# Attention-value product of one core: 128-query chunks as two 64-column halves, value tiles with rows of 72 instead of 66 elements

## The chip, the core and the metric

The kernel runs on one core of one Trainium2 chip. The metric is the device time of one execution in microseconds. Before the change it is 365.22 us, the median of three runs (364.77 to 365.48). The profile that is read below is one execution with a span of 363.3 us.

The names of the engines are those of the profile: PE is TensorE's matmul side and PEld its weight loads, DVE is VectorE, ACT ScalarE, POOL GpSimd, SP the queue from which most transfers are issued.

## What is computed

Attention with pooled queries for 8 batches of 8 heads, 1152 positions, head size 64, and behind it a layer with two input matrices, a maximum and an output matrix. In the reference (cut to what matters; `B, H, S, D = 8, 8, 1152, 64`, 4608 pooled tokens):

```python
q_pool = q.reshape(B, H, S // 2, 2, D).mean(axis=3)
scores = np.matmul(q_pool, k.transpose(0, 1, 3, 2)) / np.sqrt(D)
attn = np.exp(scores - np.max(scores, axis=-1, keepdims=True))
attn = attn / (np.sum(attn, axis=-1, keepdims=True) + 1e-09)
attn_out = np.matmul(attn, v)
x = attn_out.transpose(0, 2, 1, 3).reshape(B * 576, H * D)
out = np.maximum(x @ w1, x @ w2) @ w_out
```

## The kernel before, in words

Heads are taken two at a time, which gives 32 pairs (4 per batch). For a pair the 576 pooled queries and the 1152 keys make 9 key tiles of 128 (`NT`) by 576 queries, for each of two heads. Scores are made transposed, keys on the partitions: line 738 multiplies `kT` by `qpT`, two matmuls side by side, one per head, each on 64 rows of the array, into a score tile `sps`. ACT takes the exponential of a group of 512 columns of both heads (line 745) into `et`, in bf16. No maximum is subtracted; the sum of the exponentials comes from a column of ones that stands behind the 64 value columns in `vE`.

The attention-value product of a pair is what the change touches. It is made by `av_jobs` in units of PE work, for each head (`half`):

- `chunk(half, sb)`, line 649: for 128 queries (`sb` from 0 to 3) nine matmuls, one per key tile, added up in PSUM. The stationary operand is a 128x128 piece of `et`, the moving operand the 65 columns of `vE` (64 values and the ones). The result lies on 128 partitions, queries down, 65 columns wide. There are 8 chunks in a pair, 256 in all, so 2304 matmuls.
- `rest()`, line 661: the last 64 queries of both heads. Here the stationary operand is 128x64, the one head writes PSUM partitions 0 to 63 and the other 64 to 127, so two matmuls lie beside each other in the array as two column tiles of 64. 18 matmuls per pair, 576 in all.
- `norm(half)`: DVE takes the reciprocal of the sums (line 671) and multiplies (lines 675 and 679) into `xnat`.

`vE` is filled by a POOL cast (line 549) from the loaded values; a row of it has 66 elements for one head and key tile, of which 65 are read.

PE's other work in the same stretch of time is the maxout layer, whose weights are turned into a difference `wd` and a product `w21`: line 952 (`xT` by `wd`), line 985 (output product, pairs of matmuls on 64 rows each), and at the end lines 925 and 1018, the same products with all 128 rows. Lines 870, 569, 585, 618, 800 and 841 are small products and transposes; lines 464 and 473 are matmuls on a constant that keep PE busy.

A planner places all of this. Its costs and due times make a first order, but what is emitted comes from strings written out by hand, one letter for each unit, one string for each of PE, DVE, POOL and SP (`pe_order` and the others, from line 1577). Every unit waits for the semaphores of what it reads and of the bank that it writes. The planner's modes name how the array is cut up: `f` for the whole array, `s` for two row halves, `c` for two column halves, `z` for quarters. The mode of `chunk` is `f` and that of `rest` is `c`; the change leaves these words and the strings alone.

Of the kernel before, what the change touches and what calls it, by code (L numbers as in the profile page):

```python
# [8 lines left out]
BF16 = mybir.dt.bfloat16  # L9
P = 128  # L10
# [344 lines left out]
def bass_funnel_attn__then__act_maxout2_kernel(  # L355
# [13 lines left out]
    NT = S // P  # L369
    HP = P // 2  # L370
# [23 lines left out]
    with outer:  # L394
        def sbuf(shape, dt, name):
            return room.enter_context(nc.sbuf_tensor(name, list(shape), dt))
# [12 lines left out]
        qpT = [sbuf([P, SQ], BF16, f"qpT{s}") for s in range(3)]  # L409
        kbf = [sbuf([P, NT, 2, D], BF16, f"kbf{s}") for s in range(2)]  # L410
        kT = [sbuf([P, NT, P], BF16, f"kT{s}") for s in range(3)]
        vE = [sbuf([P, NT, 2, 66], BF16, f"vE{s}") for s in range(3)]
        et = sbuf([P, 4 * PW], BF16, "et")
        et2 = et[:, :].rearrange("p (h c) -> p h c", h=2)
        rcs = sbuf([P, NPAIR, 2 * NCH + 1], FP32, "rcs")
# [18 lines left out]
        fb = [w[:, half, :] for w in wide for half in range(2)]  # L434
# [4 lines left out]
        def rows(half):  # L439
            return slice(half * HP, half * HP + HP)  # L440
# [112 lines left out]
        def unit(r, cost, go, mode="f"):  # L553

            def plan_it(m):
                op("PE", lambda e: go(e, m), r=r, w=[f"f{m}"], cost=cost, mode=mode)
            return r, plan_it, cost, mode

        def dve(fn, r, w, cost):
            op("DVE", fn, r=r, w=w, cost=cost)  # L560
# [73 lines left out]
        def av_jobs(i):  # L634
            b, h0 = i // NHP, 2 * (i % NHP)
            es = i % 2
            vs = i % 3
            xs = b % 2
            need = [f"et{es}.{g - first(i)}" for g in range(first(i), after(i))] + [f"vE{vs}", f"v.{i}"]

            def col(half, t, sb):
                return (half * 2 + es) * PW + flat(i, t, sb * P)

            def chunk(half, sb):

                def go(e, m):
                    for t in range(NT):
                        a = col(half, t, sb)
                        last = e.matmul(  # L649
                            fb[m][:, sb * 66:sb * 66 + 65], et[:, a:a + P],  # L650
                            vE[vs][:, t, half, 0:65], start=(t == 0), stop=(t == NT - 1))
                    return last
                return unit(need, 0.2755, go)

            def rest():

                def go(e, m):
                    for t in range(NT):
                        for half in range(2):
                            a = col(half, t, NCH)  # L660
                            last = e.matmul(  # L661
                                fb[m][rows(half), NCH * 66:NCH * 66 + 65], et[:, a:a + NB],
                                vE[vs][:, t, half, 0:65], start=(t == 0), stop=(t == NT - 1))
                    return last
                return unit(need, 0.308, go, "c")

            def norm(half):
                def evac(m):
                    n = NCH + 1 - half
                    a = fb[m][:, 0:(NCH + 1) * 66].rearrange("p (j c) -> p j c", c=66)  # L670
                    dve(lambda e: e.reciprocal(rcs[:, i, half * (NCH + 1):half * (NCH + 1) + n], a[:, 0:n, 64]),  # L671
                        [f"f{m}"], [f"rc{half}"], 0.19)
                    if half == 0:
                        for k in range(2):
                            dve(lambda e, k=k: e.tensor_tensor(
                                xnat[xs][rows(0), i % NHP, NCH, k * D:k * D + D], a[rows(k), NCH, 0:D],
                                rcs[rows(k), i, NCH:NCH + 1].to_broadcast([HP, D]), ALU.mult),
                                [f"f{m}", "rc0"], [f"xr{xs}.{h0 + k}"], 0.221)
                    dve(lambda e: e.tensor_tensor(
                        xnat[xs][:, i % NHP, 0:NCH, half * D:half * D + D], a[:, 0:NCH, 0:D],  # L680
                        rcs[:, i, half * (NCH + 1):half * (NCH + 1) + NCH].unsqueeze(2).to_broadcast([P, NCH, D]), ALU.mult),
                        [f"f{m}", f"rc{half}"], [f"xn{xs}.{h0 + half}", f"f{m}"], 0.425)
                return evac

            return [Job("a", ([] if half else [rest()]) + [chunk(half, sb) for sb in range(NCH)],
                        norm(half), nb=i) for half in range(2)]

        def first(i):

            return i * PW // W  # L690

        def after(i):
            return -(-(i + 1) * PW // W)
# [4 lines left out]
        def flat(i, t, lo):  # L698

            at = 0  # L700
            for a, z in runs(i):
                if lo < z:
                    return at + t * (z - a) + lo - a
                at += NT * (z - a)
# [959 lines left out]
```

## Time and profile before

| | |
|---|---|
| median of 3 runs | 365.22 us |
| span of the profiled execution | 363.3 us |
| PE busy, matmuls | 354.4 us (98%), 5973 |
| PE weight loads | 222.3 us (61%), 5973 |
| ACT busy | 314.7 us (87%) |
| DVE busy | 242.1 us (67%) |
| POOL busy | 124.4 us (34%) |
| granted TensorE clock | 1.000 |

The median lies 1.9 us over the span, which is what the span does not hold of an execution. Matmuls overlap: a matmul of 65 columns is listed with some 0.19 us although the next starts about 0.03 us after it, so the pace of a row of matmuls is read from first start to last start, and not from the mean of one. A row "start, length, xN" of the timeline covers the N instructions from the first start to the end of the last.

### The profile page before, as it was taken

The numbers are of one execution on the slowest core, as the hardware profiler recorded it, in microseconds if no ns is written. First come the engines' busy times: TensorE is split into PE (matmuls) and PEld (weight loads), VectorE is DVE, ScalarE is ACT, GpSimd is POOL, SyncE is SP. The second block draws the span as 40 slices with busy tenths as digits, with TensorE's granted clock in tenths as the row PEclk, the third lists the DMA queues.
The fourth block names the chain that finished last, engine by engine and source line by source line (L and its number), as shares of the span: only waits on it lengthen the run. The fifth ranks groups of instructions, "written<-read, shape, count | busy, mean of one in ns | idle before, by whom it ended". The sixth has DMA issues, their size and how long they took to land.

```text
span 363.3 us, 13384 instructions
## 1 busy us (share of the span) xinstructions
PE 354.4 (98%) x5973; PEld 222.3 (61%) x5973; DVE 242.1 (67%) x526; ACT 314.7 (87%) x355; POOL 124.4 (34%) x111
## 2 busy tenths in 40 slices
PE   7998999999999999999999999999999999999995
PEld 6675655666564666657575665666666566656842
DVE  2777468877589777948968595676977847715421
ACT  4999999989999999999999999999999989894221
POOL 1246986344045433452251604613424320010000
PEclk9999999999999999999999999999999999999999
DMA  7999999999859998996999999986999570723106
GB/s 261 403 395 396 403 278 325 233 311 308 212 98 265 280 291 248 232 267 152 315 297 210 239 298 299 294 258 161 249 252 241 162 163 12 190 47 68 41 6 174
DMA packets 77790, 84.78 MB, mean 233 GB/s; under 512 B 50080, under 2 KB 50848, under 8 KB 77728
## 3 DMA queue, kind: packets, MB, share of 16 engines
q1 hardware_dynamic: 77168, 83.09, 85.8%
q8 instruction: 48, 0.79, 0.9%
q10 hardware_dynamic: 560, 0.79, 0.7%
q14 instruction: 14, 0.11, 0.1%
HBM read 62.91 MB, written 9.44 MB: 199 GB/s over the span
## 4 chain that ended last, share of the span: by engine, by line
PE 89%; ACT 7%; DMA 1%; issue 0%; SPq 0%; POOL 0%; DVE 0%; DVEq 0%
PE sps L738 20%; PE sps L649 13%; PE sps L985 11%; PE fb L985 10%; PE sps L952 9%; ACT et L745 7%; PE fb L649 7%; PE fb L952 7%; PE sps L1018 3%; PE sps L661 2%; PE fb L870 2%; PE fb L1018 1%; PE sps L925 1%; DMA kraw<-in_k_dram 1%; PE fb L661 1%; PE fb L925 1%
## 5 line engine op out<-in xcount | busy, mean ns | idle before, releaser
L745 ACT ACTIVATE et<-sps 128x1024 bf16<-128x1024 f32 (+1 forms) x336 | 306.7, 1006 | 19.7 <-PE sps L738 17.8
L738 PE MATMUL sps<-qpT,kT 64*128 64x256 bf16 (+7 forms) x1162 | 118.4, 283 | 0.7 <-ACT et L745 0.3
L603 DVE STREAM_TRANSPOSE qpT<-qp 32x288 bf16<-32x288 bf16 x216 | 101.4, 469 | 5.6 <-PE sps L738 1.5
L738 PEld LDWEIGHTS sps<-qpT,kT 64*128 64x128 bf16 x1162 | 47.9, 94 | 48.4 <-ACT et L745 16.3
L543 POOL TENSOR_TENSOR qp<-qraw 128x576 bf16<-128x576 f32 x30 | 42.1, 1405 | 89.6 <-DVE qpT L603 66.0
L549 POOL TENSOR_SCALAR vE<-vraw 128x1152 bf16<-128x1152 f32 x32 | 36.8, 1151 | 65.8 <-DMA vraw<-in_v_dram 63.4
L649 PE MATMUL sps<-vE,et 128*128 128x65 bf16 x1368 | 48.6, 193 | 0.4 <-issue 0.4
L649 PEld LDWEIGHTS sps<-vE,et 128*128 128x128 bf16 x1368 | 43.7, 97 | 6.5 <-issue 5.6
L510 POOL TENSOR_SCALAR kbf<-kraw 128x1152 bf16<-128x1152 f32 x31 | 35.6, 1151 | 33.4 <-DMA kT<-kbf 16.8
L952 PE MATMUL sps<-xT,wd 64*128 64x512 bf16 (+3 forms) x368 | 43.4, 326 | 0.0
L985 PE MATMUL sps<-wo,stage 64*128 64x512 bf16 x256 | 36.8, 376 | 0.0
L952 PE MATMUL fb<-xT,wd 64*128 64x512 bf16 (+3 forms) x272 | 33.5, 333 | 0.1
L649 PE MATMUL fb<-vE,et 128*128 128x65 bf16 x936 | 33.1, 193 | 0.0
L985 PE MATMUL fb<-wo,stage 64*128 64x512 bf16 x224 | 33.0, 376 | 0.0
L649 PEld LDWEIGHTS fb<-vE,et 128*128 128x128 bf16 x936 | 29.8, 97 | 4.8 <-issue 4.1
L961 DVE TENSOR_SCALAR stage<-sps 128x1024 bf16<-128x1024 f32 (+3 forms) x23 | 22.3, 969 | 15.4 <-PE sps L952 15.2
L961 DVE TENSOR_SCALAR stage<-fb 128x1024 bf16<-128x1024 f32 (+3 forms) x17 | 17.0, 999 | 10.7 <-PE fb L952 10.4
L952 PEld LDWEIGHTS sps<-xT,wd 64*128 64x128 bf16 x368 | 15.6, 94 | 13.5 <-PE sps L952 1.4
L671 DVE RECIPROCAL rcs<-sps 128x5 f32<-128x5 f32 (+1 forms) x38 | 7.0, 185 | 20.0 <-PE sps L649 19.5
L985 PE MATMUL sps<-w,xT 64*128 64x512 bf16 x128 | 18.8, 376 | 0.0
L996 DVE COPY stage<-sps 128x1024 f32<-128x1024 f32 x8 | 9.8, 1225 | 12.8 <-PE sps L985 12.7
L985 PEld LDWEIGHTS sps<-wo,stage 64*128 64x128 bf16 x256 | 12.1, 94 | 9.5
(88 smaller groups left out, 292.9 us busy)
## 6 DMA issues: line engine op xcount, KB each, us to landing
vraw<-in_v_dram SPq DMA_DIRECT2D x32, 576.0 KB, 6.6
kraw<-in_k_dram SPq DMA_DIRECT2D x31, 576.0 KB, 6.3
qraw<-in_q_dram SPq DMA_DIRECT2D x31, 576.0 KB, 6.1
out_dram<-stage SPq DMA_DIRECT2D x21, 256.0 KB, 5.8
out_dram<-stage SPq DMA_DIRECT2D x23, 128.0 KB, 3.3
xT<-in_moe_w_dram SPq DMA_DIRECT2D x4, 512.0 KB, 10.3
stage<-in_moe_w_out_dram SPq DMA_DIRECT2D x4, 512.0 KB, 14.0
stage<-in_moe_w_dram SPq DMA_DIRECT2D x4, 512.0 KB, 13.7
```

What stands on the lines that cost most here:

```text
L510: op("POOL", lambda g: g.tensor_scalar(kbf[s][:, :, :, :].rearrange("p t h d -> p h t d"), kraw[r][:, :, :, :], 1.0, 1.0, ALU.mult, ALU.mu ...
L543: op("POOL", lambda g: g.tensor_tensor(qpf[s][:, :, :], qraw[r][:, :, 0, :], qraw[r][:, :, 1, :], ALU.add), r=[f"qraw{r}"], w=[f"qp{s}.0", ...
L549: op("POOL", lambda g: g.tensor_scalar(vE[r][:, :, :, 0:D].rearrange("p t h d -> p h t d"), vraw[r][:, :, :, :], 1.0, 1.0, ALU.mult, ALU.m ...
L603: op("DVE", lambda e: e.transpose(view[dst:dst + 32, :, 32 * pb:32 * pb + 32], qpf[s][src:src + 32, :, 32 * db:32 * db + 32]), r=[f"qp{s}. ...
L649: last = e.matmul(fb[m][:, sb * 66:sb * 66 + 65], et[:, a:a + P], vE[vs][:, t, half, 0:65], start=(t == 0), stop=(t == NT - 1))
L661: last = e.matmul(fb[m][rows(half), NCH * 66:NCH * 66 + 65], et[:, a:a + NB], vE[vs][:, t, half, 0:65], start=(t == 0), stop=(t == NT - 1))
L738: last = e.matmul(sps[r][:, h, col:col + hi - lo], kT[i % 3][rows(h), t, :], qpT[i % 3][rows(h), lo:hi], start=True, stop=True)
L745: op("ACT", lambda e: e.activation(et2[:, :, c:c + z - a], sps[r][:, :, a - g * W:z - g * W], EXP, scale=scale), r=[f"s{r}"], w=keys + ([f ...
L952: last = e.matmul(fb[m + k][:, 0:size], wd[z, ct, (f0 + k) * P:(f0 + k + 1) * P], xT[z, ct, n0:n1], start=(turn == 0 and ct == 0), stop=(t ...
L961: dve(lambda e: e.tensor_scalar_max(gT[:, f0:f0 + 2, g0:g0 + size], wide[m // 2][:, :, 0:size], 0.0), [f"f{m}", f"f{m + 1}"], w + [f"f{m}" ...
L985: last = e.matmul(fb[m + k][:, :], lhs, rhs, start=(turn == 0 and j == 0), stop=(turn == 1 and j == NC_ + NF - 1))
L1018: return e.matmul(fb[m][:, 0:c1 - c0], lhs, rhs[:, c0:c1], start=(j == 0), stop=(j == NC_ + NF - 1))
```

## The change

```diff
-        vE = [sbuf([P, NT, 2, 66], BF16, f"vE{s}") for s in range(3)]
+        vE = [sbuf([P, NT, 2, 72], BF16, f"vE{s}") for s in range(3)]
...
                     for t in range(NT):
                         a = col(half, t, sb)
-                        last = e.matmul(
-                            fb[m][:, sb * 66:sb * 66 + 65], et[:, a:a + P],
-                            vE[vs][:, t, half, 0:65], start=(t == 0), stop=(t == NT - 1))
+                        for k in range(2):
+                            last = e.matmul(
+                                fb[m][rows(k), sb * 66:sb * 66 + 65], et[:, a + k * HP:a + k * HP + HP],
+                                vE[vs][:, t, half, 0:65], start=(t == 0), stop=(t == NT - 1))
                     return last
                 return unit(need, 0.2755, go)
```

`HP` is 64 and `rows(k)` is partitions 64k to 64k + 63. Each matmul of a chunk becomes two: the stationary operand is split into two halves of 64 queries, the moving operand is the same for both, and the halves write the lower and the upper 64 partitions of the same columns. The PSUM layout, and so all that DVE reads, stays as it was. A row of `vE` takes 72 elements; 65 of them are read as before. Every line behind the edit has a number one higher.

On PE, early in the program (a rest unit and five chunks of a pair, then scores, then three chunks), the order before was

```order
L661 MATMUL sps<-vE,et 64x65 x18
L649 MATMUL sps<-vE,et 128x65 x45
L738 MATMUL sps<-qpT,kT 128x64 x2
L738 MATMUL sps<-qpT,kT 128x448 x2
L738 MATMUL sps<-qpT,kT 128x128 x2
L738 MATMUL sps<-qpT,kT 128x384 x2
L649 MATMUL sps<-vE,et 128x65 x27
```

and it is now

```order
L662 MATMUL sps<-vE,et 64x65 x18
L650 MATMUL sps<-vE,et 64x65 x90
L739 MATMUL sps<-qpT,kT 128x64 x2
L739 MATMUL sps<-qpT,kT 128x448 x2
L739 MATMUL sps<-qpT,kT 128x128 x2
L739 MATMUL sps<-qpT,kT 128x384 x2
L650 MATMUL sps<-vE,et 64x65 x54
```

Nothing changes places; twice as many matmuls stand in a chunk's row, and they have the shape of the rest's.

On PE near the end, where single matmuls of line 925 (whole array) stand between chunks of the last pair, the order before was

```order
L661 MATMUL sps<-vE,et 64x65 x18
L925 MATMUL sps<-xT,wd 128x128
L649 MATMUL sps<-vE,et 128x65 x45
L925 MATMUL sps<-xT,wd 128x128
L649 MATMUL sps<-vE,et 128x65 x18
L925 MATMUL fb<-xT,wd 128x128
L649 MATMUL sps<-vE,et 128x65 x9
L1018 MATMUL sps<-w,xT 128x512 x3
```

and it is now

```order
L662 MATMUL sps<-vE,et 64x65 x18
L926 MATMUL sps<-xT,wd 128x128
L650 MATMUL sps<-vE,et 64x65 x90
L926 MATMUL sps<-xT,wd 128x128
L650 MATMUL sps<-vE,et 64x65 x36
L926 MATMUL fb<-xT,wd 128x128
L650 MATMUL sps<-vE,et 64x65 x18
L1019 MATMUL sps<-w,xT 128x512 x3
```

Here too the places are the same, but a chunk now has another shape than the matmul of line 926 beside it. The rows of DVE, ACT, POOL and SP, and what they wait for, are the same in both.

## The prediction, as put on record before the run

> **What bounds the kernel now.** I read the page first: the span, the engines' shares and the chain of work that ended last.
>
> ```profile
> span 363.3 us, 13384 instructions
> PE 354.4 (98%) x5973; PEld 222.3 (61%) x5973; DVE 242.1 (67%) x526; ACT 314.7 (87%) x355; POOL 124.4 (34%) x111
> PE 89%; ACT 7%; DMA 1%; issue 0%; SPq 0%; POOL 0%; DVE 0%; DVEq 0%
> ```
>
> A busy PE proves little, since matmuls overlap, but the chain runs over PE for 89% of the span. Where its other 7% lie, the chain in order of time tells:
>
> ```profile
> 7.68 0.67 PE fb L464 x12
> 8.35 0.34 PE sps L738 x4
> 8.69 0.02 issue
> 8.71 26.76 ACT et L745 x30
> 35.47 0.05 issue
> 35.52 0.39 PE sps L738 x4
> 35.91 0.86 PE fb L870 x8
> ...
> 39.65 0.41 PE sps L661 x18
> 40.05 1.46 PE sps L649 x45
> 41.52 0.54 PE sps L738 x8
> 42.06 0.93 PE sps L649 x27
> ```
>
> From 8.7 to 35.5 us the exponentials set the pace and PE waits for them; from 35.9 us on the chain names ACT no more, so PE's order alone sets the end. The waits of PE's matmuls agree:
>
> ```profile
> PE sps L738 <- ACT et L745: 0.3, 2, 0.2
> ```
>
> So there is no slack behind 35.9 us in which a longer PE stretch could vanish: what a chunk gains or loses there goes to the end one for one. Before it, it costs nothing. How many of the chunk matmuls lie on either side (first row before, second behind; PE time, then PEld):
>
> ```profile
> 0.00:35.90 35.90, 5.57 (x144) 4.77 (x144) 1.00 0.97 363
> 35.90:363.30 327.40, 76.16 (x2160) 68.76 (x2160) 1.00 0.86 219
> ```
>
> 240 of the 256 chunks count. The clock granted to PE is 1.00 in both stretches, and I take it to stay there.
>
> **The change part by part.** Nothing changes its place in any engine's order, and no wait is added; the sum is one of PE's pace.
>
> *Today's pace.* The shortest, middle and longest matmul of both kinds, and stretches of the timeline:
>
> ```profile
> L649 PE MATMUL sps<-vE,et x1368: 190/192/204, 40.0 to 334.4; 128*128 128x65 bf16 x196
> L661 PE MATMUL sps<-vE,et x342: 192/195/218, 39.6 to 332.0; 128*64 128x65 bf16 x171
> ...
> 290.30 2.35 PE L649 MATMUL fb<-vE,et 128*128 128x65 bf16 x72
> ```
>
> 72 matmuls take 2.35 us less the last one's 0.19, over 71 steps: 30.4 ns from start to start. Over all: the order of the program has 70 unbroken rows of chunk matmuls on PE, 7 of them in the first 36 us. The 63 others hold 76.16 us less 63 x 0.192, 64.1 us, in 2160 - 63 = 2097 steps: 30.5 ns a step, start-up of a row included.
>
> *The new pace.* The trace already has the new form: the rest unit of line 661 (18 matmuls in two column tiles of 64, 65 moving columns). One of them, cut off after 47.20 us and whole, and the chunk behind it:
>
> ```profile
> 47.14 0.25 PE L661 MATMUL sps<-vE,et 128*64 128x65 bf16 x4
> ...
> 47.14 0.47 PE L661 MATMUL sps<-vE,et 128*64 128x65 bf16 x18
> 47.54 0.24 PE L649 MATMUL sps<-vE,et 128*128 128x65 bf16 x2
> ...
> 35.90:363.30 327.40, 14.22 (x540) 10.95 (x540) 1.00 0.86 219
> ```
>
> The fourth matmul ends at 47.39 and so began at 47.19: the second pair starts 53 ns after the first, a start-up. The 30 rest units behind 35.9 us (last row) hold 14.22 us, 0.474 each, less 0.195 for the last matmul: 0.279 us from first to last start. Less the start-up of 0.053 and the 0.004 that the two of a pair lie apart, 0.222 us remain for 7 pairs: **31.9 ns a pair**, which now does what one step of 30.5 did. A bound from below is today's 30.5; one from above takes the start-up into the pace, 0.275 / 8 = 34.4. I take 31.9, as this is the same instruction, tile and moving size.
>
> - Steps: 2097 x (31.9 - 30.5) = +2.9 us.
> - Start-up: of the 63 rows 23 stand right behind a rest unit, which already has the new form; 40 start anew, 40 x (53 - 32) ns = +0.8 us.
> - Between rest and chunk the array now keeps its form. Today the last rest matmul of the row above starts at 47.415 (47.14 + 0.47 - 0.195) and the chunk at 47.54, 125 ns; from then on 32 - 4 = 28. 23 x 97 ns = -2.2 us. One chunk row stands ahead of a rest unit, -0.1 us.
> - Six borders between chunks and whole-array matmuls become changes of form. Three are these:
>
> ```profile
> 331.68 0.47 PE L661 MATMUL sps<-vE,et 128*64 128x65 bf16 x18
> 332.08 0.23 PE L925 MATMUL sps<-xT,wd 128*128 128x128 bf16 x1
> 332.15 1.52 PE L649 MATMUL sps<-vE,et 128*128 128x65 bf16 x45
> 333.51 0.22 PE L925 MATMUL sps<-xT,wd 128*128 128x128 bf16 x1
> 333.56 0.71 PE L649 MATMUL sps<-vE,et 128*128 128x65 bf16 x18
> 334.11 0.22 PE L925 MATMUL fb<-xT,wd 128*128 128x128 bf16 x1
> 334.17 0.43 PE L649 MATMUL sps<-vE,et 128*128 128x65 bf16 x9
> 334.44 0.81 PE L1018 MATMUL sps<-w,xT 128*128 128x512 bf16 x3
> ```
>
>   From chunk to line 925 it is 0.03 us today (333.56 + 0.71 - 0.19 to 334.11), from rest to line 925 0.12 (331.96 to 332.08): 6 x 0.1 = +0.6 us.
> - The second matmul of the last pair starts 4 to 5 ns later, 58 times ahead of other work: +0.3 us.
>
> The sum is 2.9 + 0.8 - 2.2 - 0.1 + 0.6 + 0.3 = **+2.3 us**, 363.3 to 365.6 us in the profiled execution; the median stood 1.9 us above that span, so 365.2 + 2.3 = **367.5 us**. With the bounds of the pace, 30.5 and 34.4 ns (start-up then within it), the sum is -0.6 and +6.8: 364.6 to 372.0.
>
> Edits at nothing. The padding: POOL casts into rows of `vE` in as much time as into the dense rows of `kbf`, and had 63.4 us of waiting for the loads of `vE` alone, which a slower cast would use up first.
>
> ```profile
> L549 POOL TENSOR_SCALAR vE<-vraw 128x1152 bf16<-128x1152 f32 x32 | 36.8, 1151 | 65.8 <-DMA vraw<-in_v_dram 63.4 <-PE sps L649 2.4
> L510 POOL TENSOR_SCALAR kbf<-kraw 128x1152 bf16<-128x1152 f32 x31 | 35.6, 1151 | 33.4 <-DMA kT<-kbf 16.8 <-DMA kraw<-in_k_dram 13.5 <-PE sps L738 3.0
> q8 instruction: 48, 0.79, 0.9%
> ```
>
> For PE the row length changes the step between key tiles, 264 to 288 bytes, and no count of elements; nothing in the trace prices it, and I let it lie within the bounds of the pace. The 4608 added PE instructions (half matmuls, half loads) have to be fetched: 48 packets serve today's 11946, so some 18 more, a third of a per cent of the DMA engines' time. DVE reads the same PSUM columns.
>
> The trace bears most on the weight load. A load of 64 columns is listed in line 661 just before each matmul, and pairs follow in 32 ns. [...]
>
> **The rivals.**
>
> *A. PE's sequencer can't feed the stream.* A chunk now needs four instructions in 32 ns, 8 ns each. A rest unit shows that pace, but for 36 instructions only, which may have stood ready. The longest dense stretch is that of the fence with line 925: 93 matmuls, 186 instructions from 331.68 to 334.44 us, 14.8 ns each. If PE is fed no faster than that, a pair takes 59 ns. There are 69 unbroken stretches of attention-value work behind 35.9 us, with 2430 pairs; if the first 9 pairs of each go at 32, the other 1809 lose 27 ns each, +49 us on top of the 2.3: 416 us. Feeding at 11.4 ns, halfway, adds 25: 392 us. From 8 ns on it costs nothing. For it: no long stream of this kind stands in the trace. Against it: the 14.8 is what was asked for there, not a limit that was hit. [...]
>
> *B. Loads bind in long rows.* If the 53 ns of the first two pairs came back whenever loads can't be pulled ahead, each pair would cost 53: 2097 x 21 ns more, +44 + 2.3, 411 us. Against it speak all 30 rest units behind their first pair.
>
> *C. Faster.* The two halves of a pair read the same moving row, where a rest's two read different ones, and rows are now 144 bytes apart. If that lets a pair go at 30.0 ns, the steps give -1.0 and the rest of the sum -0.6: 363.6 us. It decides below 30.8 ns, where the steps' loss equals the saved changes of form. For it: today's single step is 30.5 with the same moving columns. Against it: line 569's transposes are pairs of the same kind on dense rows of 64, and 18 of them also took 0.47 us:
>
> ```profile
> 31.23 0.47 PE L569 MATMUL fb<-ident,qp 64*64 64x64 bf16 x18
> ```
>
> *D. No change,* with a pair at 30.5 to 31.2 ns: 364.6 to 365.9 us.
>
> **How the numbers follow.** Forecast, a pair near 32 ns, 366 to 372 us: 0.62. A 0.16, B 0.04, C 0.10, D 0.08. The predicted time is the forecast's, 367.5 us. A difference of 0.2%, 0.7 us, is about what a measurement can tell from none. Faster 0.10, same 0.08, slower 0.82. The range has to reach into A, whose times spread from 372 to 416: 364.2 to 381 us leaves out some 0.07 below (most of C) and 0.14 above.
>
> **What would show it.** Right: a chunk row of 90 matmuls at 1.44 us from first to last start (45 pairs of 32 ns); rest and chunk 28 ns apart instead of 126; ACT still off the chain behind 36 us. A shows as a row whose first pairs come every 32 ns and whose later ones come further apart, the longer the row the worse; B as 53 ns from the second pair on; C as a pair below 31. The step most likely wrong is that a pace read over 9 pairs holds for 45. The forecast falls altogether if ACT or a transfer comes back onto the chain behind 36 us.

## The result, and the profile after

The changed kernel takes 426.85 us, the median of 6 runs (418.33 to 431.74); the kernel before took 365.35 us (6 runs, 364.58 to 369.25). The ratio is 1.153, with a 95% interval of 1.148 to 1.158: 15% slower, where +2.3 us had been forecast. (The ratio leaves out runs more than 1.5% above the fastest of their kernel, the profiled one among them, and so lies below the ratio of the medians, 1.168.)

The page of the changed kernel: span, engines, PE and its granted clock in 40 slices, the queue that brings instructions, the chain of waits, and the groups of the exponentials and the chunks (busy us, mean ns, then idle time ahead of them and what ended most of it).

```profile
span 426.9 us, 17992 instructions
PE 376.8 (88%) x8277; PEld 235.5 (55%) x8277; DVE 242.7 (57%) x526; ACT 318.3 (75%) x355; POOL 124.5 (29%) x111
PE   8877999599899979989949988979797969999996
PEclk9998999889899999999999999989988988999999
q8 instruction: 66, 1.08, 1.1%
PE 84%; issue 10%; DMA 2%; ACT 1%; SPq 1%; DVE 1%; DVEq 0%
L746 ACT ACTIVATE et<-sps 128x1024 bf16<-128x1024 f32 (+1 forms) x336 | 310.3, 1001 | 79.1 <-PE sps L739 77.3
L650 PE MATMUL sps<-vE,et 128*64 128x65 bf16 x2736 | 53.6, 196 | 14.3 <-issue 14.2
L650 PE MATMUL fb<-vE,et 128*64 128x65 bf16 x1872 | 38.1, 199 | 17.9 <-issue 17.9
```

The span grew by 63.6 us, from 363.3 to 426.9. PE is busy for 88% of it in place of 98%, and "issue", time in which it waited for nothing that the profile shows, rose from 0% to 10% of the chain. The chunk matmuls alone lost 32 us to it (the last two rows). The exponentials, in the page of before, were this group:

```profile
L745 ACT ACTIVATE et<-sps 128x1024 bf16<-128x1024 f32 (+1 forms) x336 | 306.7, 1006 | 19.7 <-PE sps L738 17.8
```

They now wait 77.3 us for scores in place of 17.8: ACT waits for PE more than before, and not PE for ACT.

What such an idle time looks like: the timeline of PE around 220 us.

```profile
217.31 0.61 PE L739 MATMUL sps<-qpT,kT 64*128 64x256 bf16 x8
217.85 1.08 PE L650 MATMUL fb<-vE,et 128*64 128x65 bf16 x56
222.48 1.64 PE L650 MATMUL fb<-vE,et 128*64 128x65 bf16 x52 [3.55 <-issue]
224.05 0.61 PE L739 MATMUL sps<-qpT,kT 64*128 64x384 bf16 x4
```

And four stretches there, with PE, PEld, DVE, ACT and POOL busy, then the granted clock, the DMA share and GB/s:

```profile
215.00:218.70 3.70, 3.34 (x124) 2.47 (x125) 0.60 (x2) 1.98 (x3) 0.00 (x0) 1.00 1.26 238
218.80:222.40 3.60, 0.13 (x10) 0.02 (x2) 0.00 (x0) 0.89 (x1) 0.00 (x0) 0.95 1.23 211
222.50:225.40 2.90, 2.90 (x62) 2.12 (x64) 1.18 (x4) 0.70 (x1) 1.15 (x1) 0.50 0.02 6
225.50:231.50 6.00, 6.00 (x70) 2.88 (x66) 3.67 (x10) 5.71 (x7) 0.00 (x0) 1.00 0.01 3
```

PE stops in the middle of a row of chunk matmuls, which need no new data and no semaphore, and stands still for 3.55 us. Then it goes on at a clock of 0.50: 52 matmuls take 1.64 us, where the 56 ahead took 1.08. The clock's record has 0.50 for 3.41 us, from 222.02 us on, and then 1.00 again. So this stop costs twice, and it falls where the DMA share is 1.23.

**Where the stops lie.** I counted PE's instructions (weight loads, matmuls and the few semaphore instructions) in order of their start. Every stop of 0.5 us or more, from one start to the next, inside a row of attention-value matmuls lies at a number 193 + 256k: 705, 1217, 3009, 3265, 9153, 13249, 14273 and so on, and so do the largest stops in other work (8897, in line 986). Six more of 0.5 us or more stand at other numbers and between other lines, five of them ahead of 43 us. The instruction queue q8 moves one packet for each 256 of them: with borders at these numbers PE's 16634 instructions here make 66 blocks and the 12026 of before make 48, as many as q8 has packets (66 for 1.08 MB, 16.4 KB each, and 48), and the 18 that were added are 4608 / 256. I read the stops so that PE stands at the end of a block of 256 because the next has not come: in the four rows of after below it runs on 1.41 to 1.52 us behind the end of the next packet. The table is from the records of q8 and PE (us; "entered" is the first instruction of a block, "stop" the time from the last start ahead of it):

```
            block   entered   next packet     next block
                              begins  ends    entered   stop
after         961    27.83     31.64  32.68     34.12    3.47
after        3009    77.21     81.06  82.00     83.41    3.64
after        8897   215.36    219.95 220.96    222.48    3.74
after       14017   343.80    347.48 348.67    350.13    4.31
before       1473    43.06     46.40  47.55     49.56    0.58
before       2497    73.04     76.45  77.56     79.13    none
```

In the profile of after 30 blocks come late, with 0.3 us or more at their borders. On the mean of these, 2.72 us pass from a block's entry to the first byte of the next packet, 1.10 us while it arrives, and 1.41 us until PE runs on (1.19 to 1.56 in all 30): 5.23 us, with 3.00 to 7.14 in single blocks. PE used these 30 up in 2.03 to 6.52 us, from first start to last, and then stood for 0.34 to 4.31 us. A block that is all chunks now holds 64 pairs at 32 ns, 2.0 us; of the old form it would have held 128 matmuls at 30.5 ns, 3.9 us, and mixed with scores and maxout the old blocks lasted from 5.6 to some 10 us. The kernel before lived just above the 5.23 us. The one stop of 0.58 us in its profile stands at such a number, but this account does not cover it: its packet had landed 2.01 us before PE ran on, longer than in any of the 30, and the run with the padding alone (below) has no stop there.

The bill of the 63.6 us, in starts over all block borders: 50.5 us at borders now, 2.5 before, **48.0**. The clock is 0.50 for 34.1 us in eight stretches, which at half the rate is 17 us of lost work at most (34.1 x 0.5; pairs took 55 ns there in place of 32.2); part of it falls into the stops themselves. Each of the eight stops of 2.26 us or more has such a stretch around its end (it begins from 1.8 us ahead of it to 1.4 us behind), and no stop of 2.08 us or less has one. With 3.0 for the pace of pairs (below), **12.6** remain for the clock: a remainder within that bound, not a measurement.

### The profile page after: what moved, and what is told of

It reads as the page before. It is cut to its first block, busy times and chain, and to the rows that moved or that the text cites. A ratio compares the mean times of both kernels' runs of the same rounds, so it can differ in the third digit from the quotient of the medians.

```text
span 426.9 us, 17992 instructions
## 1 busy us (share of the span) xinstructions
PE 376.8 (88%) x8277; PEld 235.5 (55%) x8277; DVE 242.7 (57%) x526; ACT 318.3 (75%) x355; POOL 124.5 (29%) x111
## 3 DMA queue, kind: packets, MB, share of 16 engines
q8 instruction: 66, 1.08, 1.1%
## 4 chain that ended last, share of the span: by engine, by line
PE 84%; issue 10%; DMA 2%; ACT 1%; SPq 1%; DVE 1%; DVEq 0%
PE sps L739 19%; PE sps L650 11%; PE sps L986 11%; PE fb L986 9%; PE fb L650 8%; PE sps L953 8%; PE fb L953 6%; PE sps L1019 2%; DMA qraw<-in_q_dram 2%; PE sps L662 2%; PE fb L871 2%; ACT et L746 1%; PE fb L662 1%; PE fb L1019 1%; PE sps L926 1%
## 5 line engine op out<-in xcount | busy, mean ns | idle before, releaser
L746 ACT ACTIVATE et<-sps 128x1024 bf16<-128x1024 f32 (+1 forms) x336 | 310.3, 1001 | 79.1 <-PE sps L739 77.3
L739 PE MATMUL sps<-qpT,kT 64*128 64x128 bf16 (+7 forms) x1162 | 124.5, 293 | 1.7 <-issue 1.2
L739 PEld LDWEIGHTS sps<-qpT,kT 64*128 64x128 bf16 x1162 | 50.2, 96 | 50.4 <-ACT et L746 11.8
L650 PE MATMUL sps<-vE,et 128*64 128x65 bf16 x2736 | 53.6, 196 | 14.3 <-issue 14.2
L650 PEld LDWEIGHTS sps<-vE,et 128*64 128x64 bf16 x2736 | 48.0, 111 | 21.5 <-issue 21.1
L650 PE MATMUL fb<-vE,et 128*64 128x65 bf16 x1872 | 38.1, 199 | 17.9 <-issue 17.9
L650 PEld LDWEIGHTS fb<-vE,et 128*64 128x64 bf16 x1872 | 34.2, 114 | 23.5 <-issue 23.0
L953 PE MATMUL sps<-xT,wd 64*128 64x512 bf16 (+3 forms) x368 | 45.5, 335 | 0.4 <-issue 0.4
L986 PE MATMUL sps<-wo,stage 64*128 64x512 bf16 x256 | 39.8, 402 | 0.0
L672 DVE RECIPROCAL rcs<-fb 128x5 f32<-128x5 f32 (+1 forms) x26 | 4.8, 187 | 38.4 <-PE fb L650 38.3
```

Source lines behind the costliest of these rows:

```text
L650: last = e.matmul(fb[m][rows(k), sb * 66:sb * 66 + 65], et[:, a + k * HP:a + k * HP + HP], vE[vs][:, t, half, 0:65], start=(t == 0), stop= ...
L739: last = e.matmul(sps[r][:, h, col:col + hi - lo], kT[i % 3][rows(h), t, :], qpT[i % 3][rows(h), lo:hi], start=True, stop=True)
L746: op("ACT", lambda e: e.activation(et2[:, :, c:c + z - a], sps[r][:, :, a - g * W:z - g * W], EXP, scale=scale), r=[f"s{r}"], w=keys + ([f ...
L953: last = e.matmul(fb[m + k][:, 0:size], wd[z, ct, (f0 + k) * P:(f0 + k + 1) * P], xT[z, ct, n0:n1], start=(turn == 0 and ct == 0), stop=(t ...
L986: last = e.matmul(fb[m + k][:, :], lhs, rhs, start=(turn == 0 and j == 0), stop=(turn == 1 and j == NC_ + NF - 1))
```

## The experiments

Two theories stood after the result. F, fetching: doubled instructions use a block up before the next arrives. T, column tiles: the pairs of matmuls themselves (their loads, their form, the rows of 72) can't be fed or run at that pace over long rows.

**The two edits apart.** First only the rows of 72, then only the split.

```diff
-        vE = [sbuf([P, NT, 2, 66], BF16, f"vE{s}") for s in range(3)]
+        vE = [sbuf([P, NT, 2, 72], BF16, f"vE{s}") for s in range(3)]
```

> Chunks as before in whole-array matmuls, only the rows of the value tiles have 72 elements. Theory F (PE's instructions come in blocks of 256 that land too late once PE uses them faster): instruction count as before, so 365 us within 1 us and no stop of PE at a block border beyond the one of 0.6 us that the kernel before has. Rival P (the padding itself slows the value cast or PE's reads of it): most of the 60 us, over 400 us.

Measured: 365.56 us (10 runs) beside 365.30 for before (13 runs), ratio 0.9998 (0.9983 to 1.0013). The cast into the longer rows (line 549; shortest, middle and longest of 32):

```profile
L549 POOL TENSOR_SCALAR vE<-vraw x32: 1140/1151/1157, 14.9 to 319.7; 128x1152 bf16<-128x1152 f32 x32
```

1151 ns, as before: the padding costs and brings nothing.

```diff
-        vE = [sbuf([P, NT, 2, 72], BF16, f"vE{s}") for s in range(3)]
+        vE = [sbuf([P, NT, 2, 66], BF16, f"vE{s}") for s in range(3)]
```

This against the changed kernel, so that the split stands alone.

> Chunks split in two column tiles, rows of 66 elements. Theory F: 4608 more PE instructions as in the change, so 415 to 432 us, some 30 stops at block borders of about 48 us together. Rival P: 367 us. If the rows of 72 are what lets a pair of matmuls go in 31 ns, the pairs take 32 or more here.

Measured: 422.05 us (one time, as for all below unless a number of runs is given), span 420.8, clock 0.966, and 47.8 us at the block borders. The split makes the whole loss, with rows of 66 too, and the largest stops stand at the same instruction numbers (1217, 3265, 9153, 13249, 14273). The bill closes here as well: of 57.5 us in the span 45.4 lie at the borders beyond those of before, 3.0 in the pace, and the 9.1 left are within what 27.3 us at half clock can take. A pair takes 32.2 ns in its rows of 108, the same as with rows of 72.

**Less traffic.** If packets come late because data loads are ahead of them, fewer bytes must make the stops shorter, with the same instructions. From the fourth pair on, k, q and v are loaded in one slice of nine; for k, and q and v alike:

```diff
+                if i >= 3:
+                    op("SP", lambda e: e.dma_start(
+                        kraw[s][:, :, 0:1, :].rearrange("p h t d -> p h (t d)"),
+                        k[b, h0:h0 + 2, :, :].rearrange("h (p t) d -> p h (t d)", t=NT)[:, :, 0:D]),
+                        w=[f"kraw{s}"], dma=f"d_k{s}", cost=1.54)
+                    continue
```

The other slices keep what an earlier pair left there. It was done to the changed kernel and to the one before.

> The changed kernel, but from the fourth pair of heads on a load of queries, keys or values fetches a ninth of its data (the rest of the tile keeps what an earlier pair left, so the output is not the reference's); PE's instructions are the same. Theory F with the block waiting behind data transfers: the 3.7 us from asking to the first byte fall to about 1.3, a block is there some 3.8 us after it is asked for instead of 6.2, the stops shrink to under 15 us and the time falls to 370 to 385 us. Theory F with a fixed latency: 415 us or more. Rival A of the prediction (a slow pace per instruction in the sequencer): no change either, 415 us or more.

> The kernel before with the same light loads (output not the reference's). It is the reference for the run before it: both theories expect 360 to 366 us, as PE sets the end and the loads are hidden; the one stop at a block border goes if blocks wait behind data.

Measured: 383.54 us with the split, 364.38 without. The split one's page and its stretch behind 35.9 us, and that of after:

```profile
span 382.3 us, 17988 instructions
PEclk9999999999999999999999999999999999999999
q8 instruction: 66, 1.08, 1.2%
PE 90%; issue 4%; DMA 3%; ACT 2%; SPq 1%; DVE 0%; DVEq 0%
...
35.90:382.30 346.40, 331.48 (x7609) 206.24 (x7610) 223.17 (x488) 289.67 (x326) 108.31 (x89) 1.00 0.41 79
```

```profile
35.90:426.90 391.00, 348.68 (x7635) 214.10 (x7629) 224.07 (x491) 292.85 (x327) 110.97 (x92) 0.96 0.74 184
```

The DMA share falls from 0.74 to 0.41, the sum at the borders from 50.5 to 18.1 us, and the clock is 1.00 throughout; its longest stop is 1.74 us. 17 blocks are late, 5.23 us became 3.83: 1.15 to the first byte, 1.27, and 1.41 as before. Three of the 17 lie ahead of 36 us, where the loads are still full; the other 14 take 3.50, with 0.81 to the first byte. So the traffic adds some 1.6 to 1.8 us to the delay of a packet before it begins, and that makes the stops long; the other two pieces hardly depend on it. Stops were expected to fall below 15 us, and 16.2 remained in the 17: a small miss, in a time that came out as expected. With light loads the kernel before has no stop of 0.58 us (1.95 us at its borders in place of 2.5), but the run with the padding alone has none either, so this does not tell.

The pair also gives the pace by itself: 382.3 - 363.1 = 19.2 us; 18.1 - 1.95 of it lie at the borders, 16.2; **3.0** are left for all other terms of the forecast sum. These are two single runs, and runs of the kernel before lie up to 1.6 us apart (364.71 to 366.34), so 3.0 is good to about 1 us.

**The same instructions without column tiles.** Whole-array loads, each done twice, and the moving columns split instead (shown against the changed kernel; the rows of `vE` have 66 elements here):

```diff
-                    for t in range(NT):
-                        a = col(half, t, sb)
-                        for k in range(2):
+                    for c0, c1 in ((0, 33), (33, 65)):
+                        for t in range(NT):
+                            a = col(half, t, sb)
                             last = e.matmul(
-                                fb[m][rows(k), sb * 66:sb * 66 + 65], et[:, a + k * HP:a + k * HP + HP],
-                                vE[vs][:, t, half, 0:65], start=(t == 0), stop=(t == NT - 1))
+                                fb[m][:, sb * 66 + c0:sb * 66 + c1], et[:, a:a + P],
+                                vE[vs][:, t, half, c0:c1], start=(t == 0), stop=(t == NT - 1))
```

> Each matmul of a chunk becomes two as in the change, but whole-array ones: the stationary 128x128 piece is loaded twice and the moving 65 columns are cut into 33 and 32. Same 4608 added PE instructions, no column tiles. Theory F (blocks of 256 instructions land too late): PE stops at block borders as in the change, over 15 us together. If the form with two column tiles is to blame: no stops of more than 1 us in all, and only the pace of the matmuls changes. The pace itself is not known from any row: two for one take between 30 and 60 ns, 0 to 62 us, so the time (365 to 445 us) does not decide, the stops do; the slower the pair, the fewer of them.

Measured: 441.6 us. Its span, a row of 90 of its timeline, and what its matmuls of line 650 waited for (us, times, longest):

```profile
span 440.4 us, 17992 instructions
...
50.71 2.44 PE L650 MATMUL sps<-vE,et 128*128 128x33 bf16 x90
...
PE fb L650 <- issue: 9.6, 6, 2.3
PE sps L650 <- issue: 4.9, 6, 1.5
```

The stops are there without a single column tile in the chunks: 17 of them, the longest again at 1217, 9153, 13249 and 14273, with 21.9 us at the borders. The clock is 0.50 for 30.7 us, 10.2 of these from 8.3 us on, where no long stop stands. They are fewer because a block of these lasts longer: 90 matmuls in 2.44 us less 0.19 are 25 ns each, 3.2 us for 128. That step was not foreseen; it makes two half matmuls cost 50 ns in place of 30.5, 2160 x 20 = 43 us. 43 + (21.9 - 2.5) = 62 of the 77.1 us, and the rest, 15, is all that the clock can take at most (30.7 / 2), so this sum is a bound and not a proof. T falls for the stops; the experiment says nothing on the pace of column tiles.

**Half of it.** Only the second head's chunks split, 2304 instructions more:

```diff
                         a = col(half, t, sb)
+                        if half == 0:
+                            last = e.matmul(
+                                fb[m][:, sb * 66:sb * 66 + 65], et[:, a:a + P],
+                                vE[vs][:, t, half, 0:65], start=(t == 0), stop=(t == NT - 1))
+                            continue
                         for k in range(2):
```

> Only the chunks of the second head of a pair are split in two column tiles, 2304 added PE instructions in place of 4608. Theory F: stops only where a block of 256 is used up in less than some 6 us, so less than half of the change's 48 us, 8 to 22 us, and 372 to 388 us. A cost per split matmul (rival B, or a slow sequencer) would give half of the change's loss, 393 to 397 us.

Measured: 387.51 us.

```profile
span 386.2 us, 15688 instructions
q8 instruction: 57, 0.93, 1.0%
PE 91%; issue 3%; ACT 3%; DMA 1%; DVE 0%; SPq 0%; POOL 0%; DVEq 0%
```

Half of the added instructions bring 17.9 us at the borders, 15.4 more than before, a third of the 48.0 of the whole. Another 5.3 us are 55 changes of form between the two kinds of chunk, 120 to 128 ns each, some 96 ns over a step in one form. Half of the 3.0 for pace makes it 22.2 of the 22.9 us. The cost does not go with the number of instructions, as a slow sequencer's would, but with the blocks that come late: 13 here, 30 with the whole split.

**A version meant to gain.** The split was to save 2.2 us at the changes of form between rest and chunk. Splitting only the chunks that stand right behind a rest (71 of 256, 1278 instructions more) should keep that and add few instructions. `plan.cmode` is set by a rest, kept by split chunks and cleared by PE's other work:

```diff
                         a = col(half, t, sb)
+                        if not plan.cmode:
+                            last = e.matmul(
+                                fb[m][:, sb * 66:sb * 66 + 65], et[:, a:a + P],
+                                vE[vs][:, t, half, 0:65], start=(t == 0), stop=(t == NT - 1))
+                            continue
                         for k in range(2):
```

> Only the chunks that stand right behind a rest unit on PE, up to the next other work, are split: 71 of 256 chunks, 1278 added instructions. It keeps the saving of 23 changes of form (2.2 us) at a tenth more instructions. Theory F: 363.5 us if no block comes late, up to 372 if the blocks with such a row come late; the trace then shows the stops at borders inside or right behind these rows. The prediction's sum without late blocks: 363.5 to 364.5 us.

Measured: 371.84 us (6 runs, 369.05 to 374.08), before 365.20 (11 runs), ratio 1.0156 (1.012 to 1.019): 1.6% longer, less than 2% but clear of the noise, and no gain. In its profile PE around its longest stop (the first row is cut off at 191.5 us):

```profile
span 372.7 us, 14662 instructions
...
191.31 1.01 PE L655 MATMUL fb<-vE,et 128*128 128x65 bf16 x28
196.31 0.27 PE L655 MATMUL fb<-vE,et 128*128 128x65 bf16 x3 [3.98 <-issue]
196.51 0.39 PE L750 MATMUL sps<-qpT,kT 64*128 64x384 bf16 x4
```

The stop, at number 7361, falls into chunks that were not split. The block ahead of it had been used up in 4.37 us, and its successor's packet began only 6.13 us after that block's entry, later than any of the 30 (at most 4.89). So this stop, 4.17 us from start to start, is as much a late packet as a dense block; why the packet began so late is not known. 7 late blocks make 10.4 us at the borders, 7.9 more than before, and half clock for 3.41 us up to 1.7 more; of 9.4 us in the span that leaves about nothing, so whether the saved changes of form came can't be read from it. If they came they were lost to late blocks.

**Moving the borders.** If borders of blocks and not the work itself set the places, 128 more instructions at the start, which is bound by other things there, must move every stop to another piece of work. 64 matmuls on the constant were added to the changed kernel's first rows:

```diff
-                for _ in range(2 * FILL):
+                for _ in range(2 * FILL + (9 if m else 10)):
```

> The changed kernel with 64 more matmuls on a constant at the start, 128 more PE instructions, half a block. Theory F: 418 to 432 us, and every stop of over 0.3 us inside or next to attention-value work again stands at an instruction whose number on PE is 193 plus a multiple of 256, so at other units of the program than in the change. If the stops belonged to units (a wait, a bank, a transfer), they would stand at the same units, with numbers 128 higher.

Measured: 409.11 us, span 407.9, which misses the expected 418 to 432. In its timeline the stop corresponding to that of 217 us above:

```profile
208.84 1.17 PE L650 MATMUL fb<-vE,et 128*64 128x65 bf16 x61
213.22 0.66 PE L650 MATMUL fb<-vE,et 128*64 128x65 bf16 x29 [3.21 <-issue]
```

The stops stayed at 193 + 256k (8897 here, 961, 3009 and so on) and so moved to other units, as F has it: here behind 61 matmuls of a row of 90, and not 56 in a row of 108. The number of late blocks did not stay: 24 in place of 30, with 37.7 us at the borders in place of 50.5. A shift of half a block deals the dense work out over the blocks in another way, and brought the time 9 us below the fastest of the changed kernel's six runs. It is no way to mend it: 44 us are still lost.

No version was faster than the kernel before.

## Why the prediction was wrong, point by point

- **The step that failed** is the one under "Edits at nothing": "The 4608 added PE instructions (half matmuls, half loads) have to be fetched: 48 packets serve today's 11946, so some 18 more, a third of a per cent of the DMA engines' time." The 18 packets were right, and so was their share (0.9% became 1.1%). But it was priced as throughput, and it is a latency: 30 times PE stood at the end of a block, the next took 5.23 us on their mean to run, beside the full data loads, and a block now lasts as little as 2 us. That made 48.0 us at the borders and leaves some 12.6 for the half clock behind them. The profile of before had the numbers: 11946 instructions in 48 blocks over 363 us, 7.6 us on the mean, and q8's records show how long a packet takes after a border. I never compared a block's work with that.
- **"Before it, it costs nothing"**, of the stretch ahead of 35.9 us, failed with that step. PE makes its first matmul of line 870 at 34.56 us in the profile of before, and the same one (line 871) at 41.21 in that of after, 6.65 us later; the stops at 705, 961 and 1217 are 5.5 us of it. The exponentials set the pace there, but PE's stops were longer than the slack.
- **The pace held.** All terms besides the stops came to 3.0 us (the pair with light loads), where the sum gave 2.3. In the profile of after a long row, and a rest and its chunk:

```profile
233.93 1.90 PE L650 MATMUL sps<-vE,et 128*64 128x65 bf16 x108
...
216.33 0.48 PE L662 MATMUL fb<-vE,et 128*64 128x65 bf16 x18
216.64 0.74 PE L650 MATMUL fb<-vE,et 128*64 128x65 bf16 x36
```

  54 pairs in 1.90 us less 0.195: 32.2 ns over 53 steps, against 31.9 from nine pairs (0.222 us over 7 pairs is 31.7, a slip of 0.4 us in the sum; and D's upper end of 31.2 ns comes to 366.1 us, not 365.9). The step named as the most likely to be wrong, a pace read over 9 pairs, was right. From rest to chunk it is 0.03 us (216.615 to 216.64) in place of 0.125, as forecast.
- **Rival A** had about the size, 416 us, and the place, the supply of PE's instructions, but not the mechanism; the nearness of the size is luck. It put a pace on each instruction, so that long rows slow down from their tenth pair on. The row of 108 runs to its end at 7.9 ns an instruction, and the loss is in 30 whole stops at counted places. The two differ in what helps: shorter rows against A, fewer instructions in any 5 us against the other. What bounded was not the pace of issue: 7.9 ns an instruction was issued, and 48 us at the borders were not hidden.
- **Rival B** falls: at a clock of 1.00 no step from pair to pair behind the first of its row, block borders left out, took over 36 ns in the profile of after. Pairs that slow stand only at half clock: 55 ns, 52 matmuls in 1.64 us. **C and D** fall with the pace of 32.2.
- **"I take it to stay there"**, of the granted clock, failed as a consequence: it was 0.96.
- ACT stayed off the bound, as forecast, and the padding cost nothing (the first experiment).

Two things stay open. That the request for a packet goes out at about a block's entry is inferred from the times, not seen; in a few blocks the packet began ahead of the block's first start (0.68 us in the profile of after, at most 0.97 with light loads). And nothing tried has the two column tiles without added instructions, so what the tiles would be worth without the stops is known only as the +3.0 us.

## What to carry to other kernels

Count instructions as well as work: before splitting matmuls, lay the engine's instruction stream out in the blocks that its trace shows (256 here) and compare the time of the densest blocks with the time that the next packet needs (on the mean of the late blocks here 3.5 us beside light loads, 5.2 beside full ones, and up to 7.1). A cost that looked like nothing as a share of DMA time (1.1%) came to 48.0 us as a latency, so look it up from event to event, not in the table of shares. When "issue" ends idle time in the middle of a row, number the instructions: here the stops stood at 193 + 256k, also with 128 instructions added at the start, which spoke for the fetch and against the work.

## What the runs showed of the hardware beside that

- Around the end of each of the eight stops of 2.26 us or more in the profile of after the granted clock was 0.50, for 3.41 or 6.83 us, so such a stop cost up to 3.4 us more than itself (half of 6.83, an estimate). Its length alone does not decide: in other runs one of 1.67 us had it (the moving columns split), two of 2.29 and 2.37 us had not (the shifted borders), nor two of 3.06 and 3.72 us (the split alone, at 322.6 and 346.3 us).
- In rows of the run with the moving columns split a matmul of 33 or 32 columns, with a whole-array load of its own, went every 25 ns, in the kernel before one of 65 columns every 30.5: halving the columns saved about a sixth of the time.
- Where blocks begin relative to the work mattered: with 128 more instructions at the start the time was 409.1 us, where six runs without them gave 418.3 to 431.7.
